# Attention into a mixture of experts on one Trainium2 core: the gate and routing work of eight batches done in five groups

## The chip, the cores and the metric

The kernel runs on one core of a Trainium2 chip. A core has five engines that work side by side, each through its own instruction stream in order: TensorE (PE in the rows; its weight loads are PEld), VectorE (DVE), ScalarE (ACT), GpSimd (POOL) and SyncE (SP), which here issues most of the DMAs. The metric is the device time of one execution in microseconds, as the median over runs of the same program.

## The reference: what is computed

Eight batches of 12-head attention with a sigmoid in place of a softmax feed a mixture of experts with one expert per token (cut to what matters):

```python
def _attn_ref(q, k, v):                       # (8, 12, 448, 64) each
    scores = scale * np.matmul(q, k.transpose(0, 1, 3, 2)) - np.log(S)
    attn = 1.0 / (1.0 + np.exp(-scores))
    return np.matmul(attn, v)

def _moe_ref(x, w_gate, w_output_gate, w1, w2):   # x: 3584 tokens of 768, 8 experts
    logits = x @ w_gate
    e_idx = np.argmax(logits, axis=1)
    probs = softmax(logits)
    gate_w = probs[np.arange(N), e_idx]
    eom = 1.0 / (1.0 + np.exp(-(x @ w_output_gate)))
    for e in range(E):
        mask = e_idx == e
        h = np.maximum(x[mask] @ w1[e], 0.0)
        out[mask] = gate_w[mask, None] * eom[mask, e, None] * (h @ w2[e])
```

## The kernel before

**Attention.** The 8 batches have 6 pairs of heads each, and two pairs make a group `g` of the loop (24 groups). A group has 7 steps `i`, so the loop runs over u = 7 g + i up to 168. Step u issues the scores of u (`scores`, L815, 64x64 matmuls in the four corners of the array), their sigmoid on ScalarE (L817), and the value product of step u - 2 (`values`, L824). When a pair's values are complete, VectorE copies one half out of its PSUM bank (L827 for the first pair of a group, L831 for the second), adds the other half (L837) and turns the sum for the store to `x_dram` (L838). The two score banks and the four value banks are used in turn: the values of step 3 of the next group start the bank that L831 reads, and the scores of u + 2 reuse the bank that the sigmoid of u reads.

**Gates and routing.** Every third group a batch is complete. At step 3 `gates(b)` multiplies its 448 tokens by the 16 columns of the two gate matrices: for each of 6 chunks of the model dimension, four matmuls (L855), one per quarter of the tokens (128, 128, 128 and 64 tokens), each into its own 32 partitions of one PSUM bank. Then `route(b)` is stepped through at fixed places of the loop:

- right away ("logits"): VectorE turns the logits, finds the maximum and writes a one-hot of the chosen expert `oh` (L282 to L289);
- at step 0 of the next group ("counts"): ScalarE takes three sigmoids (L292 to L294), and TensorE counts how many tokens before each token chose the same expert: one product with a triangle of ones (L297), three with a full matrix of ones (L299) for the chunks before, and four (L303) for the totals;
- at step 1 ("places"): ScalarE copies the counts out (L305), VectorE takes a reciprocal (L306), and GpSimd works out each token's place in its expert's list (L307 to L312) and its gate (L313 to L317);
- at step 3 ("rows"): VectorE takes another reciprocal (L319), and GpSimd writes the tokens' rows into the lists in DRAM with four indirect DMAs (L324), each of which waits for the one before to land.

GpSimd also adds the running totals (`off`, L279) when `gates` is issued. For the last batch `gates` stands inside the first expert slot, and the routing steps are taken there.

**What stands around it.** The loop also carries the start of the expert part (`unit`): after batch 5 is routed, `table` (VectorE, L340 to L370) finds which expert the first slots take; SyncE loads w1; at u = -21 from the end SyncE loads a piece of the list (L460), which waits for the scatters of batch 5; at -18 VectorE turns it (L465), GpSimd spreads it (L469) and gathers the 8 x 128 pieces of the token rows (L509); at -11 a second list is spread; at -8 VectorE turns the gathered rows (L569, `turn_x`), and at -6, -5 and -4 they are split in a high part on ScalarE (L543) and a low part on VectorE (L544). `gates` of batch 6 stands at -18, its "counts" at -14 and its "places" at -13. The order of every engine is that of the code: a manual schedule, nothing is moved by a scheduler.

**Experts.** 14 full slots follow (first layer L587 and L588, second layer L612 to L614, in three products of high and low parts), then a slot of another width and half a slot.

The x of a finished pair is kept in six tiles of one batch (`xts`) until `gates` reads it. The routing step uses one set of small tiles `R` for all batches. `gather` and `unit` are:

```python
    def gather(self, s, rows=NT, groups=None):
        x4 = self.x_dram[0:4 * rows]
        for g in groups or range(s["lx"].shape[1]):
            self.nc.gpsimd.indirect_dma_start(...)

        if u == -18:
            self.spread_lists(self.lr_e[0], self.lts[:, 0:1], self.lxs[:, 0:1])
            self.gather(s, ROWS_E)
        ...
        if u == -8:
            self.turn_x(s)
        for k, at in enumerate((-6, -5, -4)):
            if u == at:
                self.split_x(s, k)
```

## Time and profile before

| what | value |
|---|---|
| median of 3 runs | 770.72 us (770.53 to 770.94) |
| profiled execution, its own time | 771.03 us |
| its span | 769.2 us |
| PE busy | 758.8 us (99%) |
| DVE busy | 486.5 us (63%) |
| ACT busy | 488.7 us (64%) |
| POOL busy | 349.3 us (45%) |
| share of full TensorE clock granted | 0.997 |

Attention runs to about 273 us of the span, the expert slots from there on. A busy share does not tell whether an engine is at its peak: matmul records overlap, and their ends are modelled. What an inserted piece of work costs on TensorE is therefore read from the starts of the matmuls on both sides of it, set against the same distance where nothing is inserted. The 1.8 us between the span and the profiled time lie outside the instructions that are shown.

### The profile page before, as it was taken

The numbers are of one execution on the slowest core, as the hardware profiler recorded it, in microseconds if no ns is written. First come the engines' busy times: TensorE is split into PE (matmuls) and PEld (weight loads), VectorE is DVE, ScalarE is ACT, GpSimd is POOL, SyncE is SP. The second block draws the span as 40 slices with busy tenths as digits, with TensorE's granted clock in tenths as the row PEclk, the third lists the DMA queues.
The fourth block names the chain that finished last, engine by engine and source line by source line (L and its number), as shares of the span: only waits on it lengthen the run. The fifth ranks groups of instructions, "written<-read, shape, count | busy, mean of one in ns | idle before, by whom it ended". The sixth has DMA issues, their size and how long they took to land. (4 is left out here: it accounts for less than half of the span.)

```text
span 769.2 us, 15633 instructions
## 1 busy us (share of the span) xinstructions
PE 758.8 (99%) x5973; PEld 565.6 (74%) x5973; DVE 486.5 (63%) x800; ACT 488.7 (64%) x662; POOL 349.3 (45%) x472
## 2 busy tenths in 40 slices
PE   9999999999999999999999999999999999999996
PEld 4444444444444479899999989999999999889785
DVE  3343443434356759878686676868586685877887
ACT  5666666666667846566574655747566574675685
POOL 4021303022132765787885667254372734524622
PEclk9999999999999999999999999999999999999998
DMA  6353554435359550257656597511156756397692
GB/s 263 138 218 108 182 192 157 163 140 217 109 182 336 207 158 1 63 190 230 250 184 254 178 338 278 185 54 41 43 191 208 295 159 218 125 340 258 223 411 63
DMA packets 37616, 145.22 MB, mean 189 GB/s; under 512 B 5639, under 2 KB 7791, under 8 KB 33552
## 3 DMA queue, kind: packets, MB, share of 16 engines
q1 hardware_dynamic: 27696, 119.56, 43.5%
q0 software_dynamic: 9824, 24.46, 9.3%
q8 instruction: 50, 0.82, 0.4%
q14 instruction: 46, 0.38, 0.1%
HBM read 152.61 MB, written 23.05 MB: 228 GB/s over the span
## 5 line engine op out<-in xcount | busy, mean ns | idle before, releaser
L817 ACT ACTIVATE a<-ps,bias_s 128x896 f32<-128x896 f32 x168 | 169.1, 1007 | 90.8 <-PE ps L815 90.8
L587 PE MATMUL ps<-rounded 128*128 128x512 f32 (+1 forms) x672 | 225.6, 386 | 1.2 <-PEq L999 0.9
L509 POOL DMA_INDIRECT plain<-x_dram,lxs x122 | 180.1, 1477 | 64.8 <-issue 31.1
L588 PE MATMUL ps<-rounded 128*128 128x256 f32 (+1 forms) x672 | 184.3, 274 | 0.0
L815 PE MATMUL ps<-kqv 64*64 64x448 f32 x1344 | 158.5, 543 | 0.0
L824 PE MATMUL ps<-a,kqv 64*64 64x448 f32 x1344 | 156.3, 536 | 0.0
L544 DVE TENSOR_TENSOR w2l<-plain,w2h 128x1536 fp32r<-128x1536 f32 x60 | 105.2, 1757 | 66.5 <-ACT w2h L543 61.4
L612 PE MATMUL ps<-w2h,h 128*128 128x384 f32 x432 | 145.1, 336 | 0.0
L613 PE MATMUL ps<-w2l,h 128*128 128x384 f32 x432 | 144.6, 335 | 0.0
L614 PE MATMUL ps<-w2h,h 128*128 128x384 f32 x432 | 144.6, 335 | 0.0
L587 PEld LDWEIGHTS ps<-rounded 128*128 128x128 f32 x672 | 125.9, 187 | 23.9 <-issue 2.1
L588 PEld LDWEIGHTS ps<-rounded 128*128 128x128 f32 x672 | 127.6, 190 | 0.0
L824 PEld LDWEIGHTS ps<-a,kqv 64*64 64x64 f32 x1344 | 51.5, 133 | 74.8 <-issue 73.9
L550 DVE TENSOR_TENSOR rounded<-plain,rounded 128x2048 fp32r<-128x2048 f32 x46 | 103.5, 2285 | 2.2 <-ACT rounded L547 2.2
L815 PEld LDWEIGHTS ps<-kqv 64*64 64x64 f32 x1344 | 50.2, 134 | 71.1 <-issue 67.6
L595 ACT COPY gl<-ps 128x256 f32<-128x256 f32 (+1 forms) x112 | 40.3, 359 | 95.3 <-PE ps L588 89.6
L543 ACT CAST w2h<-plain 128x1536 fp32r<-128x1536 f32 x60 | 88.2, 1474 | 16.7 <-PE ps L855 5.0
L547 ACT CAST rounded<-plain 128x2048 fp32r<-128x2048 f32 x46 | 87.2, 1902 | 0.0
L612 PEld LDWEIGHTS ps<-w2h,h 128*128 128x128 f32 x432 | 81.1, 188 | 2.3 <-issue 1.8
L613 PEld LDWEIGHTS ps<-w2l,h 128*128 128x128 f32 x432 | 81.2, 188 | 0.1
L614 PEld LDWEIGHTS ps<-w2h,h 128*128 128x128 f32 x432 | 81.1, 188 | 0.0
L634 POOL DMA_INDIRECT out<-y,due x11 | 18.2, 1655 | 112.5 <-ACT gl L595 91.7
(211 smaller groups left out, 701.2 us busy)
## 6 DMA issues: line engine op xcount, KB each, us to landing
plain<-w SPq DMA_DIRECT2D x68, 768.0 KB
plain<-w SPq DMA_DIRECT2D x48, 1024.0 KB
kqv<-kqv SPq DMA_DIRECT2D x23, 1344.0 KB
x_dram<-xt SPq DMA_DIRECT2D x8, 1344.0 KB
plain<-w SPq DMA_DIRECT2D x6, 512.0 KB
plain<-x_dram,lxs POOLq DMA_INDIRECT x122, 3.8
kqv<-kqv SPq DMA_DIRECT2D x1, 896.0 KB
lst<-plain POOLq DMA_DIRECT2D x1, 726.0 KB
```

The lines of the kernel that those rows point to most:

```text
L509: self.nc.gpsimd.indirect_dma_start(out=s["xg"][:, g], out_offset=None, in_=x4, in_offset=bass.IndirectOffsetOnAxis(ap=s["lx"][:, g:g + 1] ...
L543: self.nc.scalar.copy(hi, raw)
L544: self.nc.vector.tensor_tensor(lo, raw, r32(hi), ALU.subtract)
L550: self.nc.vector.tensor_tensor(self.w1p[1][k], self.w1r[:, 2 * k:2 * k + 2], r32(self.w1p[0][k]), ALU.subtract)
L587: nc.tensor.matmul(out, wh[d][:, c], both, start=(d == 0), stop=False)
L588: nc.tensor.matmul(ps[:, 0:n], wl[d][:, c], self.xc[:, d, 0, 0:n], start=False, stop=(d == 5))
L612: nc.tensor.matmul(ps, hh[:, f, tk], wh, start=(f == 0), stop=False)
L613: nc.tensor.matmul(ps, hh[:, f, tk], wl, start=False, stop=False)
L614: nc.tensor.matmul(ps, hl[:, f, tk], wh, start=False, stop=(f == 7))
L815: nc.tensor.matmul(ps[half[h], j, 0:S], kg[half[j], e, 0, o:o + 64], kg[half[j], e, 1], start=True, stop=True)
L817: nc.scalar.activation(at[u % 4], ps[:, :, 0:S], AF.Sigmoid, bias=self.bias_s, scale=1.0 / math.sqrt(D))
L824: nc.tensor.matmul(self.ps_o[e][h][half[j], 0:S], v[half[h], 6 if i == 3 else 3 * e + c, j], a[half[h], j], start=(i in ((0, 3 if h else 4 ...
```

## The change

The eight batches are routed in five groups: batches 0 to 2 together, 3 and 4 together, then 5, 6 and 7 alone (`GROUPS`). A quarter is now 112 tokens, so the four column strips of `gates` are of equal length, and one matmul carries all batches of a group: 336, 224 or 112 columns. The x of the grouped batches lies side by side in the big buffer `plain`, in parts that the expert phase fills later. As 112 is not a multiple of the 32-token chunks, the last chunk of each quarter has 16 places without a token; a small table `bad` adds a large number there, so that no expert is chosen and the scatter drops the row (`bounds_check`).

The counts take two matmuls for the whole group: a triangle (now with -1 in it) over all chunks, and a full matrix of ones over all chunks, written expert by expert. The sum over the chunks before is made by a scan on VectorE (L329 of the new code), which restarts at each expert by a tile `ahead` of ones with a zero at each expert's start. GpSimd writes `ahead` with two memsets (L304, L305) when `gates` is issued, ahead of `off`; it adds the scan's result (L331) and `bad` (L334) on the way to the places. The memsets of `lg` and `oh` at the start are gone; `bad` is made there instead.

The diff, cut to its core:

```diff
-QT = 32 * NCH
+QT = S // 4
+GROUPS = ((0, 3), (3, 2), (5, 1), (6, 1), (7, 1))
...
-        nc.gpsimd.memset(self.tri, 1.0)
-        nc.gpsimd.affine_select(self.tri, self.tri, pattern=[[1, 128]], compare_op=ALU.is_gt, fill=0.0,
+        nc.gpsimd.memset(self.tri, 0.0)
+        nc.gpsimd.affine_select(self.tri, self.tri, pattern=[[1, 128]], compare_op=ALU.is_gt, fill=-1.0,
...
+        self.bad = t("bad", [128, NCH])
+        for q in range(4):
+            g.iota(self.bad[32 * q:32 * q + 32], pattern=[[32, NCH]], base=-QT, channel_multiplier=1,
+                   allow_small_or_imprecise_dtypes=True)
+        g.tensor_scalar(self.bad, self.bad, 0.0, float(OOB), ALU.is_ge, ALU.mult)
...
-    def route(self, b):
+    def route(self, b, nb):
...
+        g.memset(R["ahead"], 1.0)
+        g.memset(R["ahead"][:, :, 0:1], 0.0)
         tt(self.off, self.run, self.ebase, ALU.add)
         yield "logits"
-        for n, c in self.spans:
-            v.transpose(R["lg"][0:n, c].rearrange("p c x -> p (c x)"), self.gp[0:n, 32 * c.start:32 * c.stop])
+        for i in range(nb):
+            v.transpose(R["lg"][:, NCH * i:NCH * i + NCH].rearrange("p c x -> p (c x)"),
+                        self.gp[:, QT * i:QT * i + 32 * NCH])
...
+        v.tensor_tensor(each(mf[:, 1]), each(mf[:, 1]), bad, ALU.add)
+        v.tensor_tensor(R["oh"], R["rk"], bc(mf[:, 1]), ALU.is_equal)
         yield "counts"
...
-        nc.tensor.matmul(pre, self.tri, oh.rearrange("p c e -> p (c e)"), start=True, stop=False)
-        for c in range(NCH - 1):
-            nc.tensor.matmul(pre[:, (c + 1) * E:].rearrange("p (c e) -> p c e", e=E), self.ones,
-                             oh[:, c:c + 1, :].broadcast_to([128, NCH - 1 - c, E]),
-                             start=False, stop=(c == NCH - 2))
-        for c in range(NCH):
-            nc.tensor.matmul(cnt, self.ones, oh[:, c, :], start=(c == 0), stop=(c == NCH - 1))
+        ps = self.mm_ps[:, 0:2 * n * E]
+        nc.tensor.matmul(by_c(ps[:, 0:n * E]), self.tri, oh, start=True, stop=True)
+        nc.tensor.matmul(by_e(ps[:, n * E:]), self.ones, oh, start=True, stop=True)
         yield "places"
-        nc.scalar.copy(R["pc"], ps[:, 0:(NCH + 1) * E])
+        nc.scalar.copy(pc, ps)
         v.reciprocal(sg[:, 1], sg[:, 1])
-        tt(R["pos"], R["pc"][:, 0:NCH * E].rearrange("p (c e) -> p c e", e=E),
-           self.off.unsqueeze(1).broadcast_to([128, NCH, E]), ALU.add)
+        v.tensor_tensor_scan(inc, R["ahead"].rearrange("p e c -> p (e c)"), pc[:, n * E:], 0.0, ALU.mult, ALU.add)
+        tt(R["pos"], by_c(pc[:, 0:n * E]), self.off.unsqueeze(1).broadcast_to([128, n, E]), ALU.add)
+        tt(R["pos"], R["pos"], by_e(inc), ALU.add)
...
+        tt(each(R["posf"]), each(R["posf"]), bad, ALU.add)
...
+        for c in range(n):
             g.indirect_dma_start(
-                out=self.lst, out_offset=bass.IndirectOffsetOnAxis(ap=R["posi"][0:n, c:c + 1], axis=0),
-                in_=meta[0:n, c, :], in_offset=None)
+                out=self.lst, out_offset=bass.IndirectOffsetOnAxis(ap=R["posi"][:, c:c + 1], axis=0),
+                in_=meta[:, c // NCH, c % NCH, :], in_offset=None, bounds_check=E * CAP - 1, oob_is_err=False)
...
-        def gates(b):
+        def gates(b, nb):
+            n = nb * QT
             for p in range(NPAIR):
                 for q in range(4):
-                    n = min(QT, S - QT * q)
-                    nc.tensor.matmul(self.gp[32 * q:32 * q + 32, 0:n], self.wg[:, p], xts[p][:, QT * q:QT * q + n],
-                                     start=(p == 0), stop=(p == NPAIR - 1))
+                    r = slice(QT * q, QT * q + QT)
+                    x = xs[b][p][:, r] if nb == 1 else both[b][p][:, :, r]
+                    out = self.gp[32 * q:32 * q + 32, 0:n]
+                    if nb > 1:
+                        out = out.rearrange("p (b s) -> p b s", b=nb)
+                    nc.tensor.matmul(out, self.wg[:, p], x, start=(p == 0), stop=(p == NPAIR - 1))
...
-            if i == 3 and g and g % 3 == 0:
-                gates(g // 3 - 1)
-                routing("logits")
+            for b, n in GROUPS[:-1]:
+                if i == 3 and g == 3 * (b + n):
+                    gates(b, n)
+                    routing("logits")
...
         self.layer1_mm(0)
-        gates(B - 1)
+        gates(*GROUPS[-1])
```

On TensorE, at the "counts" of the first routing (`oh` is the one-hot, `tri` and `ones` the two constant matrices; before it is batch 0 at group 4, in the changed kernel batches 0 to 2 at group 10, where `plain` holds the one-hot), before:

```order
L824 MATMUL ps<-a_154,kqv_149 64x448 x4
L297 LDWEIGHTS tri [waits DVE_49,Pool_49]
L297 MATMUL ps<-oh,tri 128x32 [waits Pool_49]
L299 LDWEIGHTS ones
L299 MATMUL ps<-oh,ones 128x24
L299 LDWEIGHTS ones
L299 MATMUL ps<-oh,ones 128x16
```

and in the changed kernel:

```order
L856 MATMUL ps<-a_157,kqv_154 64x448 x4
L324 LDWEIGHTS tri [waits Pool_49]
L324 MATMUL ps<-plain,tri 128x96 [waits DVE_49]
L325 LDWEIGHTS ones
L325 MATMUL ps<-plain,ones 128x12x8
L847 MATMUL ps<-kqv_155 64x448 [waits Activation_49]
```

Eight loads and products between two steps of attention have become two, on three times the columns.

On GpSimd, around the gather for the first slot and the routing of batch 6 (`lxs` holds the row numbers, `off` the lists' running ends), before:

```order
L509 DMA plain<-x_dram,lxs 128x192 [waits DMAHW6_49,DMAHW2_49,Pool_49]
L509 DMA plain<-x_dram,lxs 128x192 x6
L509 DMA plain<-x_dram,lxs 128x192 [waits DMASW1_49]
L279 TENSOR_TENSOR off<-run,ebase 128x8 [waits Pool_49]
L307 TENSOR_TENSOR pos<-pc,off 128x32 [waits Activation_49,Pool_49]
L309 TENSOR_TENSOR pos<-pos,oh 128x32 [waits DVE_49,Pool_49]
```

and in the changed kernel:

```order
L532 DMA plain<-x_dram,lxs 128x192 [waits DMASW1_49]
L304 MEMSET ahead 128x32 [waits Pool_49]
L305 MEMSET ahead 128x8 [waits Pool_49]
L306 TENSOR_TENSOR off<-run,ebase 128x8
L330 TENSOR_TENSOR lg<-lg,off 128x32 [waits Activation_49,Pool_49]
L331 TENSOR_TENSOR lg<-lg 128x32 [waits DVE_49,Pool_49]
```

The two memsets of `ahead` stand behind the eight gathers, and one more addition, which waits for VectorE, stands in the chain.

On VectorE, at the "places" of batch 6 (`xh` is the copied half of a pair, `lg` now also holds the counts and the scan), before:

```order
L306 RECIPROCAL sg<-sg 128x32 [waits Activation_49]
L831 COPY xh<-ps 128x448 [waits PE_49]
L837 TENSOR_TENSOR gl_111<-xh,ps 128x448 [waits DVE_49]
L838 STREAM_TRANSPOSE xt_162<-gl_111 128x14x32 [waits DVE_49]
L544 TENSOR_TENSOR rounded<-plain,rounded 128x1024 [waits DMAHW3_49,Activation_49]
```

and in the changed kernel:

```order
L328 RECIPROCAL sg<-sg 128x32 [waits Activation_49]
L329 SCALAR_TENSOR_TENSOR lg<-ahead,lg 128x32 [waits Activation_49,Pool_49]
L863 COPY xh<-ps 128x448 [waits PE_49]
L869 TENSOR_TENSOR gl_113<-xh,ps 128x448 [waits DVE_49]
L870 STREAM_TRANSPOSE xt_167<-gl_113 128x14x32 [waits DVE_49]
L567 TENSOR_TENSOR rounded<-plain,rounded 128x1024 [waits DMAHW3_49,Activation_49]
```

The scan, shown as L329, has come between the reciprocal and the copy of the next pair, and it waits for GpSimd as well as ScalarE.

## Rows read from the trace of the kernel before

**Rows 1.** The page: span, and TensorE's granted clock in 40 slices (tenths).
```profile
span 769.2 us, 15633 instructions

```

**Rows 2.** Waits of PE: line waited at, releaser, us in total, times, longest.
```profile
PE ps L587 <- DVE gl L596: 0.3, 1, 0.3
```

**Rows 3.** Timeline of PE around the first gates: start us, us, instruction, count.
```profile
41.13 0.93 PE L824 MATMUL ps<-a,kqv 64*64 64x448 f32 x8
...
43.43 0.98 PE L815 MATMUL ps<-kqv 64*64 64x448 f32 x8
44.23 0.93 PE L824 MATMUL ps<-a,kqv 64*64 64x448 f32 x8
...
45.74 0.93 PE L824 MATMUL ps<-a,kqv 64*64 64x448 f32 x8
```

**Rows 4.** Timeline of PE around the first counts.
```profile
48.74 0.93 PE L824 MATMUL ps<-a,kqv 64*64 64x448 f32 x8
49.61 0.19 PE L297 MATMUL ps<-oh,tri 128*128 128x32 bf16 x1
49.65 0.22 PE L299 MATMUL ps<-oh,ones 128*128 128x24 bf16 x3
...
49.90 0.98 PE L815 MATMUL ps<-kqv 64*64 64x448 f32 x8
50.70 0.93 PE L824 MATMUL ps<-a,kqv 64*64 64x448 f32 x8
```

**Rows 5.** Timeline of POOL: first slot's gather, then batch 6's routing; a memset.
```profile
6.19 0.12 POOL L266 MEMSET oh<- 128x32 bf16 x1
...
247.57 1.01 POOL L509 DMA_INDIRECT plain<-x_dram,lxs  x1 [0.15 <-POOL lts L472]
...
257.61 0.95 POOL L509 DMA_INDIRECT plain<-x_dram,lxs  x1 [0.30 <-issue]
258.62 0.20 POOL L279 TENSOR_TENSOR off<-run,ebase 128x8 f32<-128x8 f32 x1
258.89 0.25 POOL L307 TENSOR_TENSOR pos<-pc,off 128x32 f32<-128x32 f32 x1
259.22 0.25 POOL L309 TENSOR_TENSOR pos<-pos,oh 128x32 f32<-128x32 f32 x1
```

**Rows 6.** Timeline of DVE from batch 6's places to the turn of the gathered rows.
```profile
252.39 0.35 DVE L306 RECIPROCAL sg<-sg 128x32 f32<-128x32 f32 x1
253.42 0.62 DVE L831 COPY xh<-ps 128x448 f32<-128x448 f32 x1 [0.68 <-PE ps L824]
...
260.64 1.74 DVE L569 STREAM_TRANSPOSE plain<-plain 128x1536 f32<-128x1536 f32 x1
```

**Rows 7.** Timeline of PE and ACT behind it: values, split, sigmoid, scores.
```profile
258.43 0.93 PE L824 MATMUL ps<-a,kqv 64*64 64x448 f32 x8
...
262.65 0.61 ACT L543 CAST rounded<-plain 128x512 fp32r<-128x512 f32 x1
...
263.25 1.01 ACT L817 ACTIVATE a<-ps,bias_s 128x896 f32<-128x896 f32 x1
...
265.19 0.93 PE L815 MATMUL ps<-kqv 64*64 64x448 f32 x8
```

**Rows 8.** Busy us (and count) of PE, PEld, DVE, ACT, POOL; clock; DMA: two stretches.
```profile
254.04:262.38 8.34, 8.34 (x96) 3.40 (x92) 6.36 (x11) 6.20 (x7) 6.50 (x18) 1.00 0.45 152
...
297.00:324.00 27.00, 26.73 (x155) 24.75 (x153) 25.01 (x70) 15.00 (x22) 19.48 (x17) 1.00 0.10 27
```

**Rows 9.** Timeline of DVE: the turn of the first list.
```profile
244.94 0.51 DVE L465 STREAM_TRANSPOSE lt<-plain 32x192 f32<-32x192 f32 x1
```

**Rows 10.** Waits for the lists' scatters, of POOL and of SP's queue: total, times, longest.
```profile
POOL lst L324 <- DMA lst<-meta,posi: 46.3, 23, 4.2
SPq L460 <- DMA lst<-meta,posi: 4.8, 1, 4.8
```

93 lines of the change are left out of this document (57 added, 36 removed).

## The prediction

> **What bounds the kernel now.** I read the page first: TensorE holds its full clock in all but the last of 40 slices [rows 1]. Then the list of waits: TensorE hardly waits for anybody; the one wait in the expert slots is 0.3 us, for VectorE [rows 2]. So the time is the sum of what TensorE is given, and a piece of work taken off it is worth its full insertion cost, as long as nothing new makes it wait. What gates and counts cost is read from the timeline of TensorE: from one value product to the next takes 45.74 - 44.23 = 1.51 us where nothing is inserted, and 44.23 - 41.13 = 3.10 us across a gate [rows 3], so a gate costs 1.59 us. Across the counts it is 50.70 - 48.74 = 1.96 us [rows 4], so the counts cost 0.45 us. Eight of each make 16.3 us. Then I looked for what the change makes someone wait for: the timelines of GpSimd and VectorE where the routing of batch 6 meets the gather for the first slot [rows 5, 6].
>
> **Gates, a gain of 2.2 us.** An undisturbed step of 1.51 us is four rounds of 448 columns (scores and values, each recorded twice per matmul, four at a time), so 0.377 us a round or 0.84 ns a column. A gate is 12 such rounds (24 matmuls, twice, four strips at once), and the longest strip has 128 columns: 12 x 0.108 = 1.29 us, which leaves 0.30 us for the turn from one kind of matmul to the other and back. After the change a round has 336, 224 or 112 columns: 12 x 0.282 + 0.30 = 3.69 us for three batches instead of 3 x 1.59 = 4.77; 2.56 instead of 3.18 for two; 1.43 instead of 1.59 for one. That saves 1.08 + 0.62 + 3 x 0.16 = 2.2 us. The bounds: 1.7 us if the single strips save nothing, 2.6 us if a quarter of the turns goes too.
>
> The Trainium skill (TensorE: Matmul & The Clock Gate, section Back-to-back issue gap) has the spacing of narrow matmuls set by the weight load as well as by the columns. By that the strips of 112 would save nothing, and the sum below would be about 0.5 us worse. No row shows a narrower strip alone; I keep the columns.
>
> **Counts, a gain of 2.0 us.** The last seven of the eight products start from 49.65 on, and the next scores start at 49.90 [rows 4]: 0.036 us each, the turn back included. Six of eight go, 0.15 to 0.2 us; three times the columns give some 0.04 us back. I take 0.30 us for one batch, 0.32 for two, 0.34 for three: 1.56 us in place of 8 x 0.45 = 3.60, so 2.0 us. If the turn is all that counts, five turns of 0.45 remain and the gain is 1.35 us. Together 4.2 us, with 3.0 and 4.7 as ends.
>
> **What costs nothing.** The vector and scalar operations on 96 in place of 32 elements lie beside attention: one reciprocal of 32 takes 0.35 us [rows 6], and the grouped routings have four undisturbed steps, 6 us, until their counts. The twelve and eight scatters in a row wait 46.3 / 23 = 2.0 us for each other on average [rows 10], with about 1 us each to issue some 24 us for the eight, and the next routing comes 19 steps or 29 us later. If that cover went, GpSimd would be late for batch 5, where VectorE still has several us to spare.
>
> **The new wait, 3.6 us.** The scan (L329 of the new code) reads `ahead`, and `ahead` is written by two memsets which stand on GpSimd behind the eight gathers of the first slot. For batch 6 that is late. The reciprocal in front of the scan runs at 252.39 [rows 6]; the last gather leaves GpSimd at 257.61 + 0.95 = 258.56 [rows 5]. A memset of this size takes 0.12 us, and an operation that depends on the one before starts 0.33 us after it [rows 5], so `ahead` is ready between 258.8 and 259.2; I take 258.9. In the old kernel VectorE took the next pair's copy (L831) at 253.42. Now the copy, the addition, the split of w1, the second list and the turn of the gathered rows are all queued behind the scan. The scan is bounded by 0.1 and the reciprocal's 0.35 us; with 0.25 the copy ends near 259.8 (0.62 us long).
>
> First step of the wait: the values at 258.43 [rows 7] start the bank that this copy reads. They would come 0.3 us earlier (0.16 saved on batch 6's gate, 0.15 on its counts), at 258.1. So TensorE waits 1.7 us.
>
> Second step: VectorE has 6.36 us of work between the end of the copy, 254.04, and the end of the turn, 262.38 [rows 6, 8], and did it with 2 us of gaps. Late, it does it without: the turn ends at 259.8 + 6.4 = 266.2. ScalarE then takes the split (0.61 us), and behind it, in its order, the sigmoid of step 162 (1.01 us), which ends near 267.9 instead of 264.26. The scores of step 164 need that sigmoid's bank; they stood at 265.19 [rows 7] and with 1.4 us of delay come at 266.6. TensorE waits another 1.3 us. After that ScalarE keeps up.
>
> The start of the gather may also slip. Batch 5 gets two more operations on GpSimd (the scan's sum and `bad`) ahead of its scatters, 2 x 0.33 us; the list load waits for those scatters (4.8 us [rows 10]), and the list's turn at 244.94 [rows 9] releases the gather. Between 0 (the loads of w1 set the landing) and 0.7 us, or a scatter's longest wait of 4.2 us [rows 10] if one more of them meets those loads; I take 0.4 us, nearest to the two operations.
>
> Last, 0.2 us in the first slots: between 297 and 324 us VectorE is busy 25.01 of 27 us [rows 8] and is the one that TensorE waits for [rows 2]. The scan there is new, and GpSimd hands the gate's sum over later; 0 to 0.7 us. Together 1.7 + 1.3 + 0.4 + 0.2 = 3.6 us.
>
> **The sum.** 771.03 us for the profiled execution, less 4.2, plus 3.6, is 770.4. The median of the runs shown is 0.3 below that execution: 770.1, and with the ends of the smaller terms I say 770.2. A measurement of this kernel can tell about 0.2% (1.5 us) from no change, so this is no change: the gain is there, and the wait at batch 6 takes it back.
>
> **Rivals.** *Only the first wait.* ScalarE's order or the gaps in VectorE's backlog may be kinder than my chain. For it: the second wait is a difference of two chains of 6 to 8 us. Price: 1.3 us less, 768.9. *No wait.* The scan finds `ahead` written. Against it: the gathers would have to leave GpSimd 4 us sooner, and their eight issues alone fill 11 us [rows 5]. Price: 770.2 less 1.7, 1.3 and 0.4, 766.8. *The change does less than it says.* The three-batch reads jump from tile to tile, and the counts are written across a bank; if that costs the lower end, the gain is 3.0 instead of 4.2 us: 771.4. *Slower: the lists land late.* If the scatters of batch 5 meet the w1 loads once more, the gather, and with it `ahead`, comes up to 4.2 us later, and each us of that is a us of TensorE. It decides from 2.5 us on; at 3 us the time is 772.8, at 4.2 it is 774.0. For it: SyncE already waited 4.8 us there. Against it: the loads do not move. *Slower: the clock.* Two waits of 1 to 2 us close together could cost TensorE its full clock; at 1.2 GHz a step of 1.51 us takes 3.0, and two such steps give 773.2. Against it: no slice of attention shows less than full clock [rows 1].
>
> The Trainium skill (TensorE: Matmul & The Clock Gate, section Why this matters for your kernels) warns of idle gaps between bursts of matmuls, after which the clock halves. No row here shows such a gap inside the work.
>
> **How the numbers follow.** Forecast 0.46; only the first wait 0.20; no wait 0.10; a smaller gain 0.08; late lists 0.12; the clock 0.04. Faster by over 0.2% (below 769.2): the two cases with less waiting, 0.30. Slower (above 772.3): the last two, 0.16. Within: 0.54. The range goes from 766.7, the case of no wait, to 772.8, where the gather is 3 us late; it leaves out half of the late lists, the clock, and what of the no-wait case lies lower, about 0.14. The likeliest case alone lies between 769.3 and 771.5.
>
> **What would show it.** In the trace of the changed kernel: value products 3.69 + 1.51 = 5.2 us apart across the first gates, and 1.8 to 1.85 across counts; at batch 6, VectorE idle for 6 us in front of L329, released by GpSimd's memset; TensorE's longest wait at the values of step 157, 1.5 to 2.5 us, for L863, and a second one at the scores of step 164, for the sigmoid. I am wrong if VectorE does not stand still there, or if the sum of TensorE's new waits is far from 3.4 us.

## The result and the profile after

The changed kernel takes 783.20 us in the median of 6 runs (780.08 to 786.09), the kernel before 771.02 us beside it (770.53 to 774.16, 6 runs). The ratio is 1.0147, with a 95% interval of 1.0128 to 1.0166: slower by 1.5%, and outside the range that was given. Of the changed kernel the profiled execution took 783.06 us, of the kernel before 771.03; the spans are 781.0 and 769.2 us [rows 1], so 11.8 us are to be found.

**The gain came.** The timeline of TensorE around the first gates (three batches at once) and the first counts; columns are start us, us, engine, line, operation:

```profile
104.41 0.93 PE L856 MATMUL ps<-a,kqv 64*64 64x448 f32 x8
...
109.60 0.93 PE L856 MATMUL ps<-a,kqv 64*64 64x448 f32 x8
...
114.11 0.93 PE L856 MATMUL ps<-a,kqv 64*64 64x448 f32 x8
...
116.00 0.93 PE L856 MATMUL ps<-a,kqv 64*64 64x448 f32 x8
```

From value product to value product it is 5.19 us across the gates and 1.89 across the counts, against 1.51 where nothing is inserted. The other groups, read the same way, give 3.69, 2.57 and 1.45 us for gates of three, two and one batch, and 0.39, 0.35 and 0.32 for their counts. That is 2.2 and 1.9 us less than in the kernel before [rows 3, 4], 4.1 us in all.

**Where the time went.** Starts of the same piece of TensorE's work in both traces:

| piece | before, us | after, us | later by |
|---|---|---|---|
| scores of step 129, in attention | 208.48 | 205.37 | -3.1 |
| second layer, first slot | 292.4 | 295.6 | 3.2 |
| first layer, third slot | 342.9 | 346.5 | 3.6 |
| its second layer | 359.6 | 367.8 | 8.2 |
| first layer, sixth slot | 442.8 | 451.4 | 8.6 |
| its second layer | 459.4 | 470.0 | 10.6 |
| first layer, eleventh slot | 609.2 | 620.0 | 10.8 |
| end of the span | 769.2 | 781.0 | 11.8 |

So three places hold nearly all: the end of attention (6.9 us, which turn a lead of some 4 into a lag of 3), one slot at 346 us (4.7) and one at 451 us (1.9); the last slots add 1 us. In the list of TensorE's waits (waiter, releaser, us in all, times, longest) the longest ones lie there:

```profile
PE ps L856 <- DVE xh L863: 4.5, 1, 4.5
PE ps L611 <- DVE rounded L573: 2.5, 2, 1.2
PE ps L611 <- DVE due L645: 1.2, 1, 1.2
```

Before, the longest in attention and in the full slots was 0.3 us for VectorE [rows 2].

**The first place.** The timeline of TensorE, VectorE and GpSimd around step 157; a bracket gives the idle time ahead and its releaser:

```profile
254.94 0.91 PE L856 MATMUL ps<-a,kqv 64*64 64x448 f32 x2
260.40 1.02 PE L856 MATMUL ps<-a,kqv 64*64 64x448 f32 x3 [4.55 <-DVE xh L863]
```

```profile
259.61 0.23 DVE L329 TENSOR_TENSOR_SCAN lg<-ahead,lg 128x32 f32<-128x32 f32 x1 [8.48 <-POOL ahead L305]
259.75 0.60 DVE L863 COPY xh<-ps 128x448 f32<-128x448 f32 x1
```

```profile
258.30 0.94 POOL L532 DMA_INDIRECT plain<-x_dram,lxs  x1 [0.30 <-issue]
259.28 0.13 POOL L304 MEMSET ahead<- 128x32 f32 x1
259.46 0.11 POOL L305 MEMSET ahead<- 128x8 f32 x1
```

This is the chain that was foreseen: the last gather, the fill of `ahead`, the scan, the copy of the pair, the values of step 157. The fill ends at 259.57 us, near the foreseen time (258.9, or 259.3 with the 0.4 us that the gather was allowed to slip). TensorE is not near its foreseen time: it comes to the bank at 254.94 us, 3.2 us earlier than the 258.1 of the forecast, and waits 4.55 us instead of 1.7. Then it is slow as well. The windows view (stretch, us; busy us and count of PE, PEld, DVE, ACT, POOL; granted clock, DMA share, GB/s):

```profile
256.00:260.00 4.00, 0.00 (x0) 0.00 (x0) 0.39 (x2) 0.26 (x1) 3.21 (x7) 0.96 0.29 81
260.00:264.00 4.00, 3.60 (x24) 1.33 (x28) 3.84 (x8) 0.42 (x1) 3.31 (x12) 0.61 0.08 22
352.00:356.00 4.00, 4.00 (x16) 3.43 (x15) 1.08 (x2) 0.73 (x3) 3.39 (x5) 0.59 1.03 418
```

After four microseconds without a matmul the granted clock is 0.61 in the next four, where the stretch around it has 1.00 before [rows 8]; from 260 to 263 us alone it is 0.50, the lower of the two levels (1.2 GHz). The page does not show such a short fall, since each of its 40 slices is some 19 us long. Its line of this clock before, in tenths of full speed, is this one, and after the change every slice has a 9:

```profile
PEclk9999999999999999999999999999999999999998
```

The step at the bank loses 4.73 us, and the one at the lower clock another 1.37. A further 0.59 us are lost later, at full clock, where the forecast had its second wait: ScalarE takes a split at 266.82 us, the sigmoid stands behind it, and the scores of step 164 start as the sigmoid ends:

```profile
267.34 1.00 ACT L849 ACTIVATE a<-ps,bias_s 128x896 f32<-128x896 f32 x1
```

```profile
268.40 1.07 PE L847 MATMUL ps<-kqv 64*64 64x448 f32 x8
```

With 0.19 us lost just ahead of the bank, this makes the 6.9.

**Why TensorE's lead did not reach the lists.** The timeline of GpSimd, batches 3 and 4, whose eight scatters (L347) now stand in a row:

```profile
188.87 1.07 POOL L347 DMA_INDIRECT lst<-meta,plain  x1 [0.58 <-POOL meta L345]
191.40 0.98 POOL L347 DMA_INDIRECT lst<-meta,plain  x1 [1.46 <-DMA lst<-meta,plain]
...
199.96 0.97 POOL L347 DMA_INDIRECT lst<-meta,plain  x1 [5.21 <-DMA lst<-meta,plain]
...
214.00 0.97 POOL L347 DMA_INDIRECT lst<-meta,plain  x1 [6.97 <-DMA lst<-meta,plain]
...
217.47 0.15 POOL L304 MEMSET ahead<- 128x32 f32 x1
...
223.96 1.07 POOL L347 DMA_INDIRECT lst<-meta,posi  x1 [0.59 <-POOL meta L345]
```

The row takes 217.48 - 188.87 = 28.6 us. A scatter follows the one before after 2.4 us where little else moves, and after 6 to 8 us where a load of q, k and v runs: the DMA engines are fully busy from 208 to 214 us. GpSimd comes to batch 5 (the fill at 217.47) only then, and the first scatter of batch 5 is issued at 223.96 us, in the kernel before at 223.70. The gathers leave at 247.45 us (before 247.57 [rows 5]), behind the turn of the first slot's list on VectorE (before at 244.94 [rows 9]):

```profile
244.78 0.52 DVE L488 STREAM_TRANSPOSE lt<-plain 32x192 f32<-32x192 f32 x1 [1.69 <-DMA plain<-lst]
```

TensorE was 3.1 to 3.5 us ahead in that stretch, and next to none of it arrived.

**The second place** is GpSimd in the first slots. Batch 7's routing ran there before too. The end of its chain and what follows, after:

```profile
295.12 1.67 POOL L330 TENSOR_TENSOR lg<-lg,off 128x32 f32<-128x32 f32 x1 [0.99 <-POOL off L306]
...
303.39 2.13 POOL L345 TENSOR_TENSOR meta<-eom,den 128x4 f32<-128x4 f32 x1
305.81 2.81 POOL L347 DMA_INDIRECT lst<-meta,posi  x1 [0.29 <-POOL meta L345]
...
339.85 0.91 POOL L521 DMA_INDIRECT hb<-lst,gl  x1 [0.30 <-issue]
```

and before:

```profile
298.73 0.53 POOL L321 TENSOR_TENSOR meta<-eom,den 128x4 f32<-128x4 f32 x1
299.55 1.21 POOL L324 DMA_INDIRECT lst<-meta,posi  x1 [0.28 <-POOL meta L321]
...
329.46 0.91 POOL L498 DMA_INDIRECT hb<-lst,gl  x1 [0.31 <-issue]
```

TensorE is 3.2 us late in this stretch, the first scatter 6.3, the gathers behind the scatters 8.8 (318.82 against 310.00), the reads of the lists `hb` 10.4. VectorE, which works in order, waits for these reads at 342 us:

```profile
342.16 0.53 DVE L488 STREAM_TRANSPOSE lt<-hb 32x192 f32<-32x192 f32 x1 [6.64 <-DMA hb<-lst,gl]
```

It waited 0.48 us for the same thing before. The splits of w1 (L573) are queued behind it, and TensorE waits for them twice:

```profile
348.93 0.39 PE L611 MATMUL ps<-rounded 128*128 128x256 f32 x1 [1.23 <-DVE rounded L573]
...
351.13 0.39 PE L611 MATMUL ps<-rounded 128*128 128x256 f32 x1 [1.23 <-DVE rounded L573]
```

Behind the second wait the clock is 0.59 from 352 to 356 us (the third row of the windows above), and 0.50 from 352 to 355 us alone. Here it fell with no standstill of several microseconds ahead of it. By the starts of the matmuls the two waits cost some 3.0 us of the slot's 4.7, and the clock some 1.5.

### The profile page after: what moved, and what is told of

Same layout as the page of the kernel before. It is cut to its first block, busy times and chain, and to the rows that moved or that the text cites. A ratio compares the mean times of both kernels' runs of the same rounds, so it can differ in the third digit from the quotient of the medians.

```text
span 781.0 us, 15169 instructions
## 1 busy us (share of the span) xinstructions
PE 761.0 (97%) x5775; PEld 563.6 (72%) x5775; DVE 483.4 (62%) x773; ACT 488.0 (62%) x650; POOL 353.3 (45%) x441
## 5 line engine op out<-in xcount | busy, mean ns | idle before, releaser
L856 PE MATMUL ps<-a,kqv 64*64 64x448 f32 x1344 | 161.1, 539 | 4.5 <-DVE xh L863 4.5
L847 PE MATMUL ps<-kqv 64*64 64x448 f32 x1344 | 162.2, 544 | 0.1
L856 PEld LDWEIGHTS ps<-a,kqv 64*64 64x64 f32 x1344 | 53.6, 134 | 79.7 <-issue 71.4
L847 PEld LDWEIGHTS ps<-kqv 64*64 64x64 f32 x1344 | 52.2, 134 | 74.6 <-issue 68.8
L573 DVE TENSOR_TENSOR rounded<-plain,rounded 128x2048 fp32r<-128x2048 f32 x46 | 103.3, 2285 | 2.2 <-ACT rounded L570 2.2
```

The lines of the kernel that those rows point to most:

```text
L573: self.nc.vector.tensor_tensor(self.w1p[1][k], self.w1r[:, 2 * k:2 * k + 2], r32(self.w1p[0][k]), ALU.subtract)
L847: nc.tensor.matmul(ps[half[h], j, 0:S], kg[half[j], e, 0, o:o + 64], kg[half[j], e, 1], start=True, stop=True)
L856: nc.tensor.matmul(self.ps_o[e][h][half[j], 0:S], v[half[h], 6 if i == 3 else 3 * e + c, j], a[half[h], j], start=(i in ((0, 3 if h else 4 ...
```

## The experiments

All ratios are against the kernel before, run beside it on the same chip; on the chip of the first four experiments that took 771.40 us (22 runs). Diffs are against the changed kernel, unless another is named. "Lost" times in attention are read from the starts of TensorE's steps, against 1.51 us a step; a step runs from its scores to the next scores.

### Without the fill: `e1_ahead_once`

```diff
+            g.memset(R["ahead"], 1.0)             # at the start, in route_tiles
+            g.memset(R["ahead"][:, :, 0:1], 0.0)
...
-        g.memset(R["ahead"], 1.0)
-        g.memset(R["ahead"][:, :, 0:1], 0.0)
```

> The changed kernel, with the two fills of the mask `ahead` made once, when the tables are laid out, and no longer at the head of each routing. Theory 1 (the fills stand behind the eight gathers in GpSimd's queue, VectorE's scan waits for them, and TensorE for the copy behind the scan): the 4.7 us stall at the values of step 157 and the 1.4 us behind it go, the next lists come early enough, and what is left is the gain of gates and counts, 4.1 us: 766.5 to 768. Theory 2 (the eight scatters of batches 3 and 4 hold up GpSimd, so that the list of the first gather lands at 239.9 us as before although TensorE is 3 to 4 us ahead; the gather's turn and all lists behind it stay late with or without the fills): the scan no longer waits, but the turn of the first gathered rows still stands at 262 to 265 us on VectorE and layer 1 of the third expert slot still loses some microseconds: 770 to 776.

Measured: 781.66 us (778.15 to 785.51), ratio 1.0124 [1.0099, 1.0149]. The wait that the forecast had at its centre is gone, and the kernel is hardly faster, so that wait is not the cause of the 12 us. In its trace the scatters of batches 3 and 4 take 33.8 us and end at 222.47, one of them after a wait of 8.35. VectorE's list of waits shows who stands for them; TensorE's shows the bill:

```profile
DVE den L343 <- POOL den L339: 8.3, 1, 8.3
```

```profile
PE ps L847 <- ACT a L849: 4.1, 3, 2.5
...
PE ps L856 <- DVE x L869: 2.7, 1, 2.7
```

VectorE's reciprocal for batch 5 (L343) waits 8.3 us for a sum that GpSimd makes behind the scatters, and the next pair's copy waits in VectorE's queue. With the fill away, the late GpSimd is met at a later place of the same routing.

### The scatters of twelve: `e2_once_3_1`

```diff
 # e1_ahead_once, and
-GROUPS = ((0, 3), (3, 2), (5, 1), (6, 1), (7, 1))
+GROUPS = ((0, 3), (3, 1), (4, 1), (5, 1), (6, 1), (7, 1))
```

> As the kernel with the fills made once, and batches 3 and 4 are gated and routed one by one, so that no more than four scatters stand in a row after the first twelve. It gives up about 0.2 us of gates (two of 1.45 for one of 2.57 us) and 0.3 us of counts. Theory 1: nothing but that is lost, 767 to 768, within 0.3% of the kernel with the fills made once. Theory 2: the list of the first gather lands earlier against TensorE, so this kernel is clearly faster than the other, by 3 us or more: 767 to 768 against 770 to 776.

Measured: 788.92 us (787.32 to 790.74), ratio 1.0220 [1.0196, 1.0244], which neither theory gave. What was overlooked is that batch 3 is now routed right behind the first three, where the changed kernel has a batch more of time. In the waits from 150 to 185 us:

```profile
DVE den L343 <- POOL den L339: 22.1, 1, 22.1
```

```profile
PE ps L856 <- DVE x L869: 14.3, 1, 14.3
```

Twelve scatters run from 123.55 to 170.19 us, and TensorE stands 14.3 us in one piece. No other step of attention waits here, the two places of `e1_ahead_once` included: with groups of one behind it, the lists are in time. A missed forecast that showed the mechanism on a larger scale: a row of scatters that is longer than the time to the next routing is paid by TensorE.

### Groups of one, fill kept: `e3_singles`; before with that wait: `e4_before_wait`

```diff
-GROUPS = ((0, 3), (3, 2), (5, 1), (6, 1), (7, 1))
+GROUPS = tuple((b, 1) for b in range(8))
```

```diff
 # against the kernel before, only in batch 6
+            g.memset(ahead, 1.0)
+            g.memset(ahead[:, :, 0:1], 0.0)
         tt(self.off, self.run, self.ebase, ALU.add)
...
         v.reciprocal(sg[:, 1], sg[:, 1])
+            v.tensor_copy(seen, ahead)
```

> The changed kernel with every batch gated and routed by itself; the fills stay at the head of each routing. Gates gain eight times 0.15 us and counts eight times 0.13 us: 2.2 us. Theory 1: the wait behind the gathers stays whole, stalls of 3 us or more at the values of step 157 and their followers: 772 to 779. Theory 2: without eight scatters in a row GpSimd is not late, the list and the gather stand against TensorE as in the kernel before, and only the first wait (some 2 us, as in the prediction) is left: 769 to 772.

> The kernel before, with one wait added: in the routing of batch 6 GpSimd fills a small table of 32 numbers a row ahead of its sum into `off`, behind the eight gathers, and VectorE copies that table after the reciprocal of `places`. Nothing else is changed; the copy's result is not used. Theory 1: the copy waits from 252.5 to 259 us, VectorE's copy of the attention sums behind it is late by 6 us, TensorE loses 2 to 4 us there, and with what follows the kernel takes 773 to 778. Theory 2: the fills are not what hurts, 771 to 772.

Measured: 774.42 us for the groups of one, ratio 1.0037 [1.0022, 1.0053], and 773.87 us for the wait alone, 1.0036 [1.0020, 1.0053]. VectorE waits 5.9 us for the fill in both. In the second, TensorE's only new wait is this:

```profile
PE ps L822 <- ACT a L824: 1.0, 1, 1.0
```

Attention loses 0.41 + 1.91 us in the first and 0.26 + 1.91 in the second. So the mechanism of the forecast is there, at 2.2 to 2.5 us, and in the other order: next to nothing at the values of step 157, nearly all behind the sigmoid. The groups of one lose a further 2.2 us in a slot at 443 us, taken up below.

### On a second chip: `e5_once_singles`, `e6_before_eight`, `e7_once_four_left_out`, `e8_singles_short`

```diff
 # e5: e1_ahead_once, and GROUPS = tuple((b, 1) for b in range(8))
 # e6, against the kernel before: the four scatters of batch 3 are issued with those of batch 4
+        todo = [(b, posi, c) for c in range(NCH)]
+        if b == 4:
+            todo = [(3, late, c) for c in range(NCH)] + todo
+        for i, at, c in todo if b != 3 else []:
...
 # e7: e1_ahead_once, and
-        for c in range(n):
+        for c in range(min(n, 4) if b == 3 else n):
 # e8: e5, and a shorter chain on GpSimd
-        tt(R["pos"], by_c(pc[:, 0:n * E]), self.off.unsqueeze(1).broadcast_to([128, n, E]), ALU.add)
-        tt(R["pos"], R["pos"], by_e(inc), ALU.add)
+        v.tensor_tensor(R["pos"], by_c(pc[:, 0:n * E]), by_e(inc), ALU.add)
+        tt(R["pos"], R["pos"], self.off.unsqueeze(1).broadcast_to([128, n, E]), ALU.add)
...
-        g.tensor_scalar(R["den"], R["den"], 1e-9, None, ALU.add)
...
+        v.tensor_scalar(R["den"], R["den"], 1e-9, None, ALU.add)
```

In `e7_once_four_left_out` the four scatters of batch 4 are left out, so its tokens reach no expert; its time is that of the kernel without these four DMAs.

> Every batch gated and routed by itself, and the two fills of `ahead` made once, at the layout of the tables. Against the run with single batches whose fills stay in the routing, only the fills differ; that one took 774.4 us. Theory 3 (twelve or eight scatters in a row hold GpSimd longer than the time to the next routing; the fills cost the 2.3 us of attention stalls seen with single batches, and the rest there is lost in the expert slots, because two more operations a batch make GpSimd's lists late): 771.5 to 772.5. Theory 1 (the fills are all that is lost): 768.5 to 769.5, the gain of single gates and counts.

> The kernel before, with one thing moved: the four scatters of batch 3 are not issued with that batch but with batch 4, so that eight stand in a row on GpSimd from about 190 us on, as in the changed kernel. Gates, counts, fills and the number of operations are those of the kernel before. Theory 3: eight scatters take 28 to 33 us, GpSimd comes to batch 5's routing 3 to 8 us late, VectorE's reciprocal of `den` waits for it with the attention copies behind it, the list of the first gather is late, and the time is 775 to 784. Theory 1: there is room for them, 771 to 772.

> The changed kernel with the fills made once, and four of the eight scatters of batches 3 and 4 left out (those of batch 4, whose tokens so reach no expert); gates stay grouped. The kernel with all eight took 781.7 us. Theory 3: the stalls of attention from step 142 on go, some 9 us, and so do those of the slots that follow from them: 768 to 772. If the eight scatters are not the cause: 778 or more.

> As single batches with the fills made once, and GpSimd's chain brought back to the length that it has in the kernel before: the sum of the prefixes with the scan's result, and the addition of 1e-9 to the denominator, are done by VectorE. Theory 3: GpSimd's lists of the slots come as in the kernel before, the 2.2 us lost at the slot around 443 us go, and the gain of gates and counts shows: 768.5 to 769.5, faster than both kernels. If the slots' loss has another cause: as the run with the longer chain, 771 to 772.5.

On this chip the unchanged kernel took 780.18 us (777.82 to 787.38, 31 runs), some 9 us more than on the first. Measured: `e5` 777.19, ratio 0.9975 [0.9944, 1.0005]; `e6` 779.85, 1.0006 [0.9980, 1.0031]; `e7` 784.63, 1.0059 [1.0016, 1.0103]; `e8` 786.67, 1.0062 [1.0031, 1.0093].

`e5` cannot be told from the kernel before. In `e6` the list is turned at 250.23 us, 5.3 us later than in the kernel before on the first chip, and the total does not show it; on a kernel that loses 9 us elsewhere this decides nothing, and it was run again on another chip (below). In `e7` batch 5's first scatter leaves at 221.28 us, and the waits of `e1_ahead_once` at steps 142 and 147 are gone; later stalls of 1.97 and 2.28 us at steps 162 and 163 stay, and so do 2.85, 0.8 and 2.1 us in three slots. The row of scatters thus accounts for the earlier stalls, and not for all. The first list of `e7` is turned at 244.47 us, as late as in the changed kernel, although batch 5's first scatter leaves 2.7 us earlier. SyncE's load of the list waits for batch 5's last scatter:

```profile
SPq L483 <- DMA lst<-meta,posi: 9.6, 1, 9.6
```

It waits 5.5 us there in the changed kernel. The loads of w1, issued from 226 to 231 us, keep the DMA engines fully busy from 230 to 240 us in `e7`, and the last scatter was issued at 234.03. That is the forecast's rival of the late lists in the form in which it was named.

`e8` shows something else. From 253 to 257 us several engines stand (ScalarE's sigmoid for 3.31 us) with a releaser that the profile gives as "remote", and the clock is down to 0.61 behind it (260 to 265 us). That says nothing on the shorter chain, which therefore went to another chip too.

### Both kernels again, and the row of eight alone: `b2_before_again`, `a2_after_again`, `e6b_before_eight`

> The kernel before, unchanged, for a trace of it beside those of this call: the last call ran where the kernel before took 780.2 us instead of 771, and no trace showed where these 9 us lie. Both theories: no difference from the kernel before; the trace says which stretch of it changes between runs, the first gather and the weights of the first slots being the candidates.

> The changed kernel, unchanged, for a trace beside that of the kernel before of the same call. Both theories: about 1.5% above the kernel before, with TensorE's longest wait at the values of step 157.

> Again the kernel before with the four scatters of batch 3 issued in a row with those of batch 4, now beside a trace of the kernel before itself. Theory 3 (the eight scatters make GpSimd late for batch 5): VectorE waits 4 to 8 us for GpSimd at the reciprocal of `den`, the list of the first gather lands 4 to 6 us later than in the kernel before of this call, and the time is 3 to 8 us longer than that kernel's. Rival (what the list chain loses is hidden behind the loads of the weights, which set the start of the slots in any case): the list is late, but the time is within 1 us of the kernel before.

Measured on a third chip, where the kernel before takes 771.24 us (25 runs): the unchanged kernel 771.10, ratio 0.9998 [0.9988, 1.0007]; the changed one 784.60, 1.0176 [1.0145, 1.0207], its longest wait again that for L863 (3.4 us), and the clock 0.50 behind it from 260 to 266.5 us; the kernel before with eight scatters in a row (the edit of `e6`) 777.38, 1.0051 [1.0021, 1.0081], three of its ten runs at 770 to 771 us and seven at 775.6 to 778.9; the trace is of one of the seven.

GpSimd's timeline in the last:

```profile
189.60 1.06 POOL L329 DMA_INDIRECT lst<-meta,plain  x1 [0.28 <-issue]
...
220.11 0.91 POOL L329 DMA_INDIRECT lst<-meta,posi  x1 [3.15 <-DMA lst<-meta,posi]
...
230.12 1.06 POOL L329 DMA_INDIRECT lst<-meta,posi  x1 [0.28 <-POOL meta L323]
```

and in the unchanged kernel on the same chip:

```profile
223.01 1.06 POOL L324 DMA_INDIRECT lst<-meta,posi  x1 [0.29 <-POOL meta L321]
```

The row of eight takes 221.02 - 189.60 = 31.4 us, the next batch's first scatter is 7.1 us late, the turn of the list 6.5 (250.58 against 244.08), TensorE waits 2.9 us at most for ScalarE and 1.4 for VectorE, which it does not otherwise, and the clock is 0.50 from 271 to 274 us. Nothing of the gates, counts or `ahead` is in this kernel: in this trace bunching the scatters alone delays the lists and makes TensorE wait. How much of its 7.1 us is a detail of the edit stays open: a conversion of batch 5 waited 3.82 us for the last scatter here, since both use one small tile.

### Groups of two: `e10_once_2_2`

```diff
 # e1_ahead_once, and
+GROUPS = ((0, 2), (2, 2), (4, 1), (5, 1), (6, 1), (7, 1))
```

> The changed kernel with the fills made once and the batches grouped as two, two and then one by one, so that the rows of eight scatters stand ahead of batches 2 and 4 and batch 5's routing finds GpSimd free. Gates and counts gain some 2.5 us. Theory 3: at most 3 us are lost at batch 4's reciprocal of `den`, batch 5's list comes 3 us earlier than in the kernel before, and the time is 8 us or more below that of the changed kernel with three and two batches, 1 us below to 3 us above the kernel before. If the row ahead of batch 5 is not the cause: within 3 us of the changed kernel.

Measured: 772.37 us (770.74 to 776.46), ratio 1.0020 [1.0007, 1.0033], 12 us less than the changed kernel beside it. It is also 9 us less than `e1_ahead_once`, from which it differs in the grouping alone (on another chip, but with the kernel before at 771.24 and 771.40 us). Here a routing of one batch with no row of eight ahead of it stands before batch 5. Batch 5's first scatter leaves at 221.29 us, 2.7 us earlier than in the first trace of the changed kernel, and the list is turned 2.5 us earlier:

```profile
242.31 0.51 DVE L488 STREAM_TRANSPOSE lt<-plain 32x192 f32<-32x192 f32 x1 [1.05 <-DMA plain<-lst]
```

TensorE's waits from 10 to 290 us are a single line:

```profile
PE ps L324 <- DVE oh L317: 0.4, 1, 0.4
```

The scores of step 167 come at 265.83 us, in `b2_before_again` at 269.01: with the fill and the late row gone, the whole gain of gates and counts is there. It is given back in the expert part, 2.4 us in the slot at 376, 1.9 in that at 442, the rest at the end (the profiled execution was the longest of its runs, 776.46 us).

### The chain of batch 7: `f1_2_2_short`, `f2_singles_short7`, `f3_2_2_short7`, `f4_before_longer7`

The edits: `f1` is `e10_once_2_2` with the shorter chain of `e8_singles_short`; `f2` is `e5_once_singles`, and `f3` is `e10_once_2_2`, each with that chain in batch 7 only; `f4` lengthens the chain of the kernel before:

```diff
 # f4, against the kernel before
+        if b == B - 1:
+            g.tensor_scalar(R["pos"], R["pos"], 0.0, None, ALU.add)
...
+        if b == B - 1:
+            g.tensor_scalar(R["posf"], R["posf"], 0.0, None, ALU.add)
```

> The grouping of two, two and ones with the fills made once, and GpSimd's chain of every routing brought back to its old length: the sum of the prefixes with the scan's result and the addition of 1e-9 are done by VectorE. Theory 4 (batch 7's longer chain makes GpSimd's lists late in the slots): the chain of batch 7 takes 7 to 8 us, the slots lose under 1 us, 767 to 769.5. Rival (the slots are bound by loads and lists at fixed times): as without the shorter chain, 771 to 773.

> Single batches, fills made once, and the shorter chain for batch 7 alone. Theory 4: the gain of 2.2 us from gates and counts shows, 768.5 to 770. Rival: 771 to 773, as the slots take it back.

> The grouping of two, two and ones, fills made once, the shorter chain for batch 7 alone. Theory 4: within 1 us of the kernel with the shorter chain in every routing, 767 to 769.5. Rival: 771 to 773.

> The kernel before, with two operations added to GpSimd's chain of batch 7 alone, each of which adds 0 to what stands there (32 and 4 elements a row). Attention is untouched. Theory 4: the first scatter of batch 7 comes 1 to 3 us later and the slots lose 0.5 to 2.5 us, 771.7 to 774. Rival: no difference, 771 to 771.5.

Measured, beside 771.34 us before (31 runs): `f1` 771.99, ratio 1.0014 [1.0003, 1.0026]; `f2` 772.06, 1.0007 [0.9996, 1.0018]; `f3` 771.99, 1.0015 [1.0002, 1.0027]; `f4` 773.21, 1.0025 [1.0015, 1.0036].

`f4` shows that the length of this chain costs. GpSimd's timeline in it:

```profile
291.14 1.68 POOL L307 TENSOR_TENSOR pos<-pc,off 128x32 f32<-128x32 f32 x1 [4.29 <-ACT pc L305]
...
299.25 2.13 POOL L325 TENSOR_TENSOR meta<-eom,den 128x4 f32<-128x4 f32 x1
301.67 2.80 POOL L328 DMA_INDIRECT lst<-meta,posi  x1 [0.28 <-POOL meta L325]
```

Two added operations of 0.30 and 0.22 us make it 10.5 us instead of 7.7 in `b2_before_again`, because the last ones slide beside VectorE's splits and take 2.13 us in place of 0.53; slots lose 0.3, 0.4 and 2.2 us, and the total is 1.9 us longer. But shortening the chain did not bring the gain to the end. In `f1` it takes 6.4 us, TensorE is 3.0 us ahead of before at 288 us and 2.4 until 423, and then one slot gives back 1.75 us (18.40 against 16.64) and the end another 1.5. The times that the chain theory gave for `f1` to `f3` were missed.

### The slot at 440 us: `f5_short_lists_later`, `f6_before_lists_later`

```diff
 # f5 against f1, f6 against the kernel before
             self.spread_lists(self.lr[5], *at(20, 4))
-            yield
-            yield
+            for _ in range(8):
+                yield
```

Twenty small operations of GpSimd for late lists then stand behind the gather of that slot, no longer ahead of it.

> The grouping of two, two and ones with the fills made once and the shorter chain in every routing, and the last two steps on the late lists (twenty small GpSimd operations and VectorE's transpose ahead of them) moved behind the gather of the sixth slot's rows. Theory 5 (those operations and the drain behind them hold the gather, which holds the slot at 440 us): that slot starts its second layer 1 to 2 us earlier, 769 to 770.5 in all, 0.1 to 0.3% below the kernel before, with the loads of the last slots taking back the rest. Rival (the gather is not what that slot waits for): 771.5 to 772.5, as without the move.

> The kernel before, with the same two steps on the late lists moved behind the same gather. Theory 5: in the kernel before the gather came just in time, its slot lost nothing, and the move changes nothing, 771 to 771.5. If it gains 1 us or more here, the gather held that kernel too.

The slot's turn of the gathered rows on VectorE in `f1`, and then in `f5`:

```profile
431.86 1.78 DVE L592 STREAM_TRANSPOSE plain<-plain 128x1536 f32<-128x1536 f32 x1 [6.97 <-DMA plain<-x_dram,lxs]
```

```profile
442.22 1.78 DVE L592 STREAM_TRANSPOSE plain<-plain 128x1536 f32<-128x1536 f32 x1 [3.38 <-DMA plain<-x_dram,lxs]
```

The wait halves, and the slot takes its 16.64 us and loses nothing: the late lists ahead of its gather held that slot in `f1`, as far as one trace of each, on two chips, can show it. The totals missed: `f5` 782.65, ratio 1.0031 [1.0003, 1.0059], and `f6` 781.93, 1.0019 [0.9998, 1.0040], on a chip where the kernel before takes 779.76. In `f5` TensorE is busy for 0.98 us of the four from 252 to 256, with no releaser named.

**Not settled.** On two of the four chips several engines stand for 3 to 10 us somewhere between 250 and 285 us, with no releaser that the profile names (10.3 us on ScalarE in `f6`), and the kernel before itself takes some 9 us more there. What that is was not found. No version was measurably faster than the kernel before; the nearest are `f2`, the same, and `e5`.

## Why the prediction was wrong

The sum was 4.2 us gained and 3.6 lost; it came out as 4.1 gained and some 16 lost.

**Gates and counts: right.** 2.2 and 1.9 us, of 2.2 and 2.0. A gate of one batch, with strips of 112 columns, costs 1.45 us, where the columns gave 1.43 and the rival, spacing by weight load, 1.59. The Trainium skill (TensorE: Matmul & The Clock Gate, section Back-to-back issue gap) gives the weight load a part in the spacing; the trace bears out the columns here.

**What costs nothing: this is the step that failed.** It set "some 24 us for the eight" against 29 us to the next routing. The 24 came from an average wait of 2.0 us over all 23 [rows 10]. That row also had the longest, 4.2, and eight in a row meet two loads of q, k and v, each of which holds one scatter for 5 to 8 us: 28.6 us in the changed kernel, 30.6 when it was run again, 31.4 in `e6b_before_eight`, 33.8 in `e1_ahead_once`. The cover had 5 us to spare by the average and none by the longest. That the grouping with this row is the main cost is shown by `e10_once_2_2`, which has no row ahead of batch 5 and takes 9 us less than `e1_ahead_once`; `e6b_before_eight` shows the row alone at work. The step even named what would come ("GpSimd would be late for batch 5"), and gave VectorE several us there; `e1_ahead_once` shows a wait of VectorE of 8.3 us at that place.

**The new wait: right in kind and place, wrong in size, for the same reason.** VectorE stood in front of L329 for the fill (8.5 us, 6 foreseen), and TensorE's longest wait is at the values of step 157 for L863. The forecast moved those values only by what batch 6 itself saves, 0.3 us, as if the lists would follow TensorE's lead of the batches before. They didn't, so the lead of 3.2 us came on top of the wait: the fill at 259.57 is near where it was expected, the values at 254.94 instead of 258.1. The second wait, at the scores of step 164, is there too, with 0.59 us of 1.3 foreseen. Where there is no lead to come on top, `e4_before_wait` measures 2.2 us for the fill's wait, of 3.0 foreseen, and most of it behind the sigmoid, not at the values. The "0.4 us" for a gather that slips was in truth some 3 us, relative to TensorE. In that sense the rival of the late lists came true, in the changed kernel mainly with another cause than it named: not batch 5's scatters among the loads of w1, but those of batches 3 and 4 among the loads of q, k and v. In `e7_once_four_left_out` the named cause is at work. Nor do the loads of w1 stand still, as the prediction had it: the first is issued at 229.82 us before, at 228.93 in the changed kernel and at 226.39 in `e10_once_2_2`.

**The clock: the rival with 0.04.** After the standstill of over 4 us the granted clock was at the lower level (0.50 from 260 to 263 us), which cost some 1.4 us in attention. The Trainium skill (TensorE: Matmul & The Clock Gate, section Why this matters for your kernels) warns of such idle gaps between bursts of matmuls, and here the trace agrees. In the slot at 346 us the fall came as the rival had it, behind two waits of 1.23 us close together, and cost some 1.5 us more. In `e1_ahead_once` the same pair of waits, at 351.36 and 353.56 us, left the clock at 1.00 (351 to 357 us), while it was 0.50 there behind a single wait of 2.5 us in attention (269.5 to 272.5 us). In `e3_singles` and `e4_before_wait` the clock stayed at 1.00 through the end of attention, and the time lost is the waits' own.

**The first slots: 0.2 us foreseen, some 5 us measured, and more behind them.** The prediction looked at VectorE there, which is busy. What comes late is GpSimd: its chain for batch 7 is longer by two operations (the scan's sum and `bad`) and a wait for VectorE's scan, grows from 7.7 to 10.7 us because the last operations are slowed beside VectorE's splits, and its queue holds the scatters, the gathers and the reads of the lists for later slots. `f4_before_longer7` costs 1.9 us by this alone, without any delay of attention. It loses 2.2 us in the sixth slot, the one at 451 us here, so for that slot the longer chain is enough, and `f5_short_lists_later` points to the lists ahead of its gather as the way.

The 4.7 us of the third slot, at 346 us, need something else. `f4_before_longer7` takes an undisturbed 16.64 us there, and so do `e6b_before_eight` and `e2_once_3_1`, whose TensorE comes to that slot 8 and 15 us late: neither the longer chain nor a late attention is enough. The slot loses time in the four traces whose groups are three, two and ones (21.4 us in `after`, 19.8, 19.8 and 19.5 us in `a2_after_again`, `e1_ahead_once` and `e7_once_four_left_out`), and in no other. In these four the first read of the lists `hb` leaves GpSimd 43.7 to 44.3 us after the first slot's second layer begins, against 37.1 us before and 40.6 to 40.8 with the other groupings and in `f4_before_longer7`. Why this grouping adds another 3 us was not found.

## What to carry to other kernels

An engine that is off the critical path and issues DMAs one by one, each waiting for the last to land, has a length that must be added up with the waits that it meets beside large loads, not with their mean, and set against the time to its next use; bunching such work removes the gaps that hid it. A lead won on the busiest engine is worth only as much as the chains of lists and gathers can follow: ask of every chain beside it whether it moves with the lead or stays at its time, since TensorE waits its whole lead for a chain that stays. And waits were paid a second time here, in the clock: once behind a standstill of 4.55 us, once behind two of 1.23.

## What the runs showed of the hardware

**Small GpSimd operations beside VectorE's splits.** GpSimd's operations on 32 partitions, 0.18 to 0.20 us otherwise, in `f1_2_2_short`, and VectorE's line of the same stretch:

```profile
396.60 2.25 POOL L494 CAST lts<-wg 32x8 int32<-32x8 f32 x1
398.80 2.25 POOL L495 COPY lts<-wg 32x8 f32<-32x8 f32 x1
401.12 2.15 POOL L492 CAST gl<-lt 32x32 int32<-32x32 f32 x1
```

```profile
396.51 6.69 DVE L573 TENSOR_TENSOR rounded<-plain,rounded 128x2048 fp32r<-128x2048 f32 x3
```

Three splits of 2.23 us each run from 396.51 to 403.20, and in that time GpSimd gets through one operation per split; the next one, at 403.22, takes 0.19 us again. The Trainium skill (SBUF — State Buffer, section Who interferes with whom) has VectorE and GpSimd share a pair of ports under an exclusive lock; the trace agrees.

**A scatter's landing.** The issue of an indirect scatter takes about 1 us in attention, beside idle and beside busy DMA engines; in the changed kernel the next one, which waits for the landing, followed 2.4 us after it in a quiet stretch (193.79 after 191.40) and 8 us after it where the DMA engines were fully busy (214.00 after 206.06, DMA share 1.00 from 208 to 214 us).

**A wait of one length on GpSimd.** In `f1`, GpSimd stands 8.02 us ahead of the gather of one slot, though its releaser had long been done. It does so for 8.02 to 8.04 us in 19 of the 20 traces here, for 8.03 at 417.9 us in the kernel before as well, so it is not of the change; what fixes this length the profile does not show.
